# Six token tiles moved through DRAM with two block buffers and three landing buffers

## The chip, the cores and the metric

One core of a Trainium2 chip runs the whole program. The metric is the device time of one execution in microseconds (us). The engines are named as in the profile: PE (TensorE, the matrix engine), DVE (VectorE), ACT (ScalarE), POOL (GpSimd), and SP, whose queue issues all the DMAs of this kernel. Each engine works through its own instructions in the order in which they were recorded, and waits for others by semaphores.

## The reference

Three stages follow each other: attention, a first feed-forward layer with a softmax-like gate and a norm, and a mixture of four experts.

```python
scores = scale * q @ k^T          # 2 batches, 8 heads, 576 tokens, 64 wide
scores = where(mask, scores, -1e9)   # heads 0-3: a window of 32; heads 4-7: every 4th of 128
x = softmax(scores) @ v           # -> 1152 tokens x 512
h = x @ w_in                      # 512 -> 1024
e = exp(h - max(h));  solu = h * e / sum(e)
ln = (solu - mean) / sqrt(var + 1e-6) * g_ln
x = ln @ w_out                    # 1024 -> 512
for e in range(4):
    out += p[:, e] * (relu(x @ w1[e]) @ w2[e])   # 512 -> 1024 -> 512
```

All of it is float32; each product is made of three products of rounded parts (high x high, high x low, low x high).

## The kernel before

The 1152 tokens are nine tiles of 128 (t = 0 to 8) and three chunks of three tiles (c = 0 to 2). The work is cut into steps, each a Python generator that records a few instructions and yields. A long string, ORDER, names the step to be resumed next, up to the middle of the first expert; after that loops record the rest. So ORDER sets the order of every engine's instructions at once, and a "+" behind a name moves a choice from one engine to another (`copy`: ACT or, with +, DVE; `pick`: DVE or, with +, POOL; the last step of `moe_H`: DVE or, with +, ACT). The names used below:

- **UD.t.b, UP.t.b** (`att_U`): a block of attention; its scores and later "PV", the product with v, are PE work (lines 262, 271 and 320). Five of them carry the probabilities to DRAM and back in between (`da<-sta`, `pt<-da`, lines 299 and 303). After PV, `xhi` and `xlo` are written.
- **VO.j.t** (`conv_out`): converts w_out into `wh` and `wl`.
- **H.t** (`moe_H`): x @ w_in for one tile, 24 products in a `pm` tile of PSUM (line 350), then maximum, exponential, a product with sums and a scaling on DVE and ACT (lines 355 to 364). `pm` has two buffers, `pa` has two more.
- **T.t** (`moe_T`, `swap_T`): turns tile t so that its 1024 features lie on the partitions, and splits it into `hh` (high part, `copy`) and `hl` (low part, `pick`). Tiles 0 to 2 are turned on PE. Tiles 3 to 8 are turned in `swap_T`: DVE transposes blocks of 32x32 into `st4` (lines 395, 397), a DMA writes them to a DRAM tile `dt` (402, 405), DMAs read them back in another order into a landing buffer `et` (411, 414), ACT sums squares of `e` (407), and `hh` and `hl` follow (170 or 172, and 419). There is one `st4`, and a landing buffer for even and one for odd tiles. Tile 5 (`ROWS`) goes by four writes and one read, the other five by one write and two reads.
- **X.c.d** (`moe_X`): ln @ w_out for one chunk and one half of the outputs, 48 products in a `pm` tile (line 432) and a copy to `xf`. ORDER cuts the two X of chunk 0 in halves of 24, called X.0.0a, X.0.0b, X.0.1a and X.0.1b here. The first product of an X reads `hh` of its three tiles, the second one `hl`. Chunk 0 is tiles 0 to 2, chunk 1 tiles 3 to 5, chunk 2 tiles 6 to 8.
- **sc** (`scales`): small operations on the row sums, one of them on POOL (line 652).
- **XQ.s, WP.g, WV.g**: sums and splits of x, w1 and w2 for the experts (line 464 and the helper lines 170 and 172); **u.s** is the upward product of an expert in seven parts p1 to p7 (line 545), **d.t** the downward one (line 617). **l...** are loads.

`end_att` closes the attention's pools and opens `xf`, the pool of the last chunk's `hh` and `hl`, and the pool `spo` with `st4` and the landing buffers in their place.

Of the kernel before, what the change touches and what calls it, by code (L numbers as in the profile page):

```python
# [40 lines left out]
UP.2.1+ UP.2.1 H.4 H.4 UP.1.1+ VO.2.1+ UP.1.1+ UD.2.1+ UP.1.1 H.4 UP.1.1+ UP.1.1 UP.1.1 UP.1.1 X.0.1+ lO.3.0 VO.3.0 lvd.2.1 UP.2.1 VO.2.1+ UP.1.1+ VO.2.0+
VO.2.0 VO.2.1+ VO.2.1+ X.0.0 VO.3.0+ VO.3.0 VO.3.0+ VO.3.0 lO.3.1 VO.3.1 VO.3.1 UD.2.1+ VO.3.1+ VO.3.1 UP.2.1 VO.3.1 VO.3.0 H.4+ VO.3.1 VO.3.0+ VO.3.1 X.0.1+
UP.2.1 UP.1.1+ UP.1.1+ UD.2.1 UD.2.1 UP.1.1+ endA T.4 X.0.1 T.4+ T.4 H.3+ T.3+ T.3+ UP.1.1+ UP.1.1 H.5+ T.4+ T.3+ T.3+ H.5+ H.5+ H.5+ H.5+ H.5 X.0.0+ X.0.0
UP.2.1+ UP.2.1+ T.5+ T.5+ T.3+ H.6+ H.6+ T.4 T.4+ T.5 H.6 H.6+ T.3+ H.8 H.6 T.6 T.5+ T.6 H.8 H.8 T.5+ H.8+ H.8 T.8+ T.8+ T.6 T.6 H.7+ H.7 H.7 H.7 H.7 T.7+
# [9 lines left out]
def fused_kernel(ctx, tc, qkp, qkd, vp, vd, w_in, w_out, gp, w1, w2, out):  # L54
    nc = tc.nc
# [335 lines left out]
    def swap_T(t, e, lh, ll):  # L391
        ef = e.rearrange("p u x -> p (u x)")
        st = spo[0].tile([128, 4, 8, 32], F32, name="st4", tag="st4")
        if t in ROWS:
            nc.vector.transpose(st.rearrange("p g q j -> p q g j"), ef.rearrange("p (q g i) -> p q g i", g=4, i=32))
        else:
            nc.vector.transpose(st.rearrange("p (u g) q j -> p q u g j", u=2), ef.rearrange("p (q u i g) -> p q u g i", u=2, g=2, i=32))  # L397
# [2 lines left out]
        if t in ROWS:  # L400
            for g in range(4):
                nc.sync.dma_start(out=dt[32 * g:32 * g + 32, :].rearrange("i (a x) -> a i x", a=4), in_=st[:, g].rearrange("p q j -> p (q j)"))
        else:
            dw = dt.rearrange("p x -> (p x)").rearrange("(u p x) -> u p x", u=2, p=128)
            nc.sync.dma_start(out=dw.rearrange("u p x -> p u x"), in_=st.rearrange("p (u g) q j -> p u (g q j)", u=2))
# [381 lines left out]
```

## Time and profile before

| | us |
|---|---|
| median of three runs | 530.44 (529.91 to 531.85) |
| the profiled execution | 530.29 |
| its span, first to last instruction | 528.5 |
| PE busy in the span | 515.0 (97%), 3971 products |
| DVE, ACT, POOL busy | 356.9, 191.7, 187.3 |

The page gives PE a busy share near 100% in all but the first of its 40 slices, and in the chain of work that ended last PE holds 87% of the span and DMAs 7%. A time in the rows below is counted from the start of the span. PE's granted clock was 1.00 from 30 us on. How to read it: the loops of the experts fill the span from about 150 us to its end, and what comes ahead of them is a mixture of attention, conversions and the first layer in which all engines wait for each other.

### The profile page before, as it was taken

To read this page: it belongs to the slowest core of one execution; us is meant where nothing else is said; L and a number is where in the kernel's file an instruction comes from. 1 tells how busy PE (TensorE), PEld (TensorE's weight loads), DVE (VectorE), ACT (ScalarE), POOL (GpSimd) and SP (SyncE) were. 2 spreads that over 40 slices of the span, in tenths; PEclk is the share of its full clock that TensorE was granted. 3 is DMA by queue.
4 is the path that set the end of the run, shared out by engine and by line. 5 is a ranking of instruction groups with operands and counts; after the bars stand their busy time and mean duration, and the time that the engine had idled before them with its cause. 6 is when DMAs were issued, how large, how long until landed. Compare 5 with 4: busy or idle time off the path is not lost.

```text
span 528.5 us, 9419 instructions
## 1 busy us (share of the span) xinstructions
PE 515.0 (97%) x3971; PEld 459.0 (87%) x3971; DVE 356.9 (68%) x474; ACT 191.7 (36%) x295; POOL 187.3 (35%) x130
## 2 busy tenths in 40 slices
PE   7799999999999999999999999999999999999997
PEld 3578898888999998998989899898989889898986
DVE  6889996777978874854685485568448656853632
ACT  3768965423254432321422232142214213312210
POOL 2554220312233532730571173048117313820300
...
GB/s 311 364 239 211 242 175 97 112 141 211 16 159 141 19 2 35 126 1 1 159 1 1 0 160 0 1 141 20 2 0 161 1 0 81 0 1 1 1 81 99
DMA packets 24490, 46.44 MB, mean 88 GB/s; under 512 B 4480, under 2 KB 9088, under 8 KB 24064
## 3 DMA queue, kind: packets, MB, share of 16 engines
...
q8 instruction: 31, 0.51, 0.4%
...
## 4 chain that ended last, share of the span: by engine, by line
PE 87%; DMA 7%; DVE 4%; ACT 1%; SPq 1%; issue 0%; DVEq 0%; ACTq 0%
PE pa L617 19%; PE pm L617 18%; PE pm L545 17%; PE pa L545 17%; PE pm L350 7%; PE pm L432 6%; DMA vp<-in_vp_dram 2%; PE pa L320 2%; DMA et<-dt 2%; DMA draw<-in_moe_w_in_dram 1%; DMA dt<-st 1%; PE pa L271 1%; DVE e L359 1%; DVE e L364 1%; PE pa L381 1%; DVE st L397 0%
## 5 line engine op out<-in xcount | busy, mean ns | idle before, releaser
L558 DVE SCALAR_TENSOR_TENSOR hl<-ct,hh 128x512 fp32r<-128x512 f32 (+1 forms) x64 | 63.6, 1012 | 35.3 <-ACT hh L556 35.3
L556 ACT ACTIVATE hh<-ct 128x512 fp32r<-128x512 f32 (+1 forms) x64 | 42.1, 682 | 48.7 <-DVE ct L588 20.7
L617 PE MATMUL pa<-wl,hh 128*128 128x512 f32 (+1 forms) x148 | 57.3, 387 | 0.0
L617 PE MATMUL pa<-wh,hh 128*128 128x512 f32 (+1 forms) x148 | 57.3, 387 | 0.0
L617 PE MATMUL pa<-wh,hl 128*128 128x512 f32 (+1 forms) x148 | 57.1, 386 | 0.0
L545 PE MATMUL pm<-xoh,hl 128*128 128x256 f32 (+1 forms) x192 | 56.8, 296 | 0.0
L545 PE MATMUL pa<-xoh,hl 128*128 128x256 f32 (+1 forms) x192 | 56.8, 296 | 0.0
L545 PE MATMUL pm<-xol,hh 128*128 128x256 f32 (+1 forms) x192 | 56.8, 296 | 0.0
L545 PE MATMUL pa<-xol,hh 128*128 128x256 f32 (+1 forms) x192 | 56.8, 296 | 0.0
L545 PE MATMUL pm<-xoh,hh 128*128 128x256 f32 (+1 forms) x192 | 56.8, 296 | 0.0
L545 PE MATMUL pa<-xoh,hh 128*128 128x256 f32 (+1 forms) x192 | 56.8, 296 | 0.0
L617 PE MATMUL pm<-wl,hh 128*128 128x512 f32 (+1 forms) x144 | 55.7, 387 | 0.0
L617 PE MATMUL pm<-wh,hh 128*128 128x512 f32 (+1 forms) x144 | 55.7, 387 | 0.0
L617 PE MATMUL pm<-wh,hl 128*128 128x512 f32 (+1 forms) x144 | 55.6, 386 | 0.0
L464 POOL TENSOR_TENSOR wl<-wl,wh 128x1024 fp32r<-128x1024 f32 x7 | 16.9, 2414 | 95.3 <-ACT wh L172 95.3
L622 DVE SCALAR_TENSOR_TENSOR xf<-pm,pr,xf 128x512 f32<-128x512 f32 (+1 forms) x32 | 23.6, 738 | 31.1 <-PE pm L617 31.1
L464 POOL TENSOR_TENSOR hl<-sw,hh 128x512 fp32r<-128x512 f32 x22 | 33.5, 1522 | 30.3 <-ACT hh L172 27.6
L622 DVE SCALAR_TENSOR_TENSOR xf<-pa,pr,xf 128x512 f32<-128x512 f32 (+1 forms) x32 | 23.6, 738 | 30.3 <-PE pa L617 30.3
L172 ACT CAST wh<-wl 128x1024 fp32r<-128x1024 f32 x16 | 16.8, 1052 | 71.0 <-PE pa L617 40.5
L572 POOL TENSOR_TENSOR ct<-ct,ct 128x512 f32<-128x512 f32 (+1 forms) x15 | 21.4, 1426 | 48.1 <-ACT ct L570 42.9
L545 PEld LDWEIGHTS pm<-xoh,hh 128*128 128x128 f32 x192 | 36.4, 190 | 0.3
L545 PEld LDWEIGHTS pm<-xol,hh 128*128 128x128 f32 x192 | 36.4, 190 | 0.3
...
## 6 DMA issues: line engine op xcount, KB each, us to landing
wl<-in_moe_w_dram SPq DMA_DIRECT2D x16, 512.0 KB, 3.7
cvr<-in_moe_w_out_dram SPq DMA_DIRECT2D x8, 512.0 KB, 3.6
rw<-in_moe_w_dram SPq DMA_DIRECT2D x8, 512.0 KB, 6.0
wh<-in_moe_w_dram SPq DMA_DIRECT2D x8, 512.0 KB
...
dt<-st SPq DMA_DIRECT2D x5, 512.0 KB, 3.3
et<-dt SPq DMA_DIRECT2D x10, 256.0 KB, 4.2
```

Source lines behind the costliest of these rows:

```text
L172: nc.scalar.copy(out, in_)
L271: nc.tensor.matmul(ps[32 * g:32 * g + 32, j, 64 * m:64 * m + 64], lhsT=qt[rows, h, xq:xq + 32], rhs=kt[rows, h, xq:xq + 64], start=False, ...
L320: nc.tensor.matmul(po[64 * (g % 2):64 * (g % 2) + 64, j, o:o + 32], lhsT=vt[rows, m, g, :], rhs=pt[rows, m, g, :], start=True, stop=True)
L350: nc.tensor.matmul(pm[:, n, :], lhsT=xx[:, kk, cols], rhs=ww["in", kk][:, 512 * n:512 * n + 512], start=(n_ == 0 and i < 2), stop=(n_ == K ...
L432: nc.tensor.matmul(pm[:, dd, 0:CW], lhsT=w_, rhs=x_[:, f, :], start=(f == 0 and i == 0), stop=(f == KF - 1 and i == 2))
L464: pick().tensor_tensor(out=out, in0=a, in1=b, op=op)
L545: nc.tensor.matmul(ps[:, ff, 0:n], lhsT=a[:, kk, fc], rhs=b[:, kk, :], start=kk == 0 and m == 0, stop=kk == 1 and m == 2)
L556: nc.scalar.activation(out=hv, in_=src, func=AF.Relu)
L558: nc.vector.scalar_tensor_tensor(out=lv, in0=src, scalar=0.0, in1=hv.bitcast(F32), op0=ALU.max, op1=ALU.subtract)
L572: poolv().tensor_tensor(out=c12, in0=c21, in1=c22, op=ALU.add)
L617: nc.tensor.matmul(po[:, 0, 0:dn], lhsT=h_[:, f, cols], rhs=w_, start=(f == 0 and i == 0), stop=(f == 3 and i == 2))
L622: nc.vector.scalar_tensor_tensor(out=acc[:, t, dc], in0=po[:, 0, 0:dn], scalar=pr[:, t, e:e + 1], in1=acc[:, t, dc], op0=ALU.mult, op1=ALU ...
```

## The change

The row form of tile 5 is dropped (`ROWS` and its branches), so that all six tiles go by one write and two reads. `st4` becomes two buffers, `st40` and `st41`, and the landing buffers become three, `et0` to `et2`; both are given out in turn, whatever the tile's number (`turn`). `st40`, `et0` and `et1` lie in a new pool `spg`, which is open from the start; `st41` and `et2` lie in `spo`. ORDER is the same up to the step T.0 of its tenth line and another from there on; the main loops are untouched. A DMA scratch area is set to 1024.

```diff
-VO.1.0+ T.0 H.1+ lvp.2.1+ UD.2.1 lO.1.1+ UD.0.1+ T.0+ T.0 UD.1.1+ H.2+ H.2+ UD.2.1+ ...
+VO.1.0+ T.0 H.1+ lvp.2.1+ UD.2.1 lO.1.1+ UD.0.1+ T.0+ UD.1.1 UD.1.1 T.0 H.2+ UD.2.1 ...
...
-    spo = [None]
+    turn = [0, 0]
+    spo = [ctx.enter_context(tc.tile_pool(name="spg", bufs=1))]
...
-        st = spo[0].tile([128, 4, 8, 32], F32, name="st4", tag="st4")
-        if t in ROWS:
-            nc.vector.transpose(st.rearrange("p g q j -> p q g j"), ef.rearrange("p (q g i) -> p q g i", g=4, i=32))
-        else:
-            nc.vector.transpose(st.rearrange("p (u g) q j -> p q u g j", u=2), ef.rearrange("p (q u i g) -> p q u g i", u=2, g=2, i=32))
+        k = turn[0] % 2
+        turn[0] += 1
+        st = spo[k].tile([128, 4, 8, 32], F32, name=f"st4{k}", tag=f"st4{k}")
+        nc.vector.transpose(st.rearrange("p (u g) q j -> p q u g j", u=2), ef.rearrange("p (q u i g) -> p q u g i", u=2, g=2, i=32))
...
-        if t in ROWS:
-            for g in range(4):
-                nc.sync.dma_start(out=dt[32 * g:32 * g + 32, :].rearrange("i (a x) -> a i x", a=4), in_=st[:, g].rearrange("p q j -> p (q j)"))
...
-        et = spo[0].tile([128, 4, 256], F32, name=f"et{t % 2}", tag=f"et{t % 2}")
-        if t in ROWS:
-            nc.sync.dma_start(out=et.rearrange("p a x -> p (a x)"), in_=dt)
...
+        k = turn[1] % 3
+        turn[1] += 1
+        et = spo[k // 2].tile([128, 4, 256], F32, name=f"et{k}", tag=f"et{k}")
...
-        spo[0] = hp1.enter_context(tc.tile_pool(name="spo", bufs=1, side="right"))
+        spo.append(hp1.enter_context(tc.tile_pool(name="spo", bufs=1, side="right")))
...
-    nc = _bacc.Bacc("TRN2", target_bir_lowering=False, num_devices=1)
+    nc = _bacc.Bacc("TRN2", target_bir_lowering=False, num_devices=1, dynamic_dma_scratch_size=1024)
```

What the new ORDER does to the engines is seen in three places. In the changed file a line stands 1 to 7 lines higher (PV 319, the first layer 349, X 425, the block write 399, the read 407).

**PE, at the end of the attention.** `pt` are probabilities and `vp` values of a PV, `pm` is the PSUM tile that a row writes. Before, X.0.1b is followed by the PVs of UP.2.1 and UP.1.1, and then by H.5:

```order
L432 MATMUL pm_1232<-hl_943,wh7_1334 128x384
L432 MATMUL pm_1232<-hh_942,wl7_1335 128x384
L320 MATMUL pa_1365<-pt_1330,vp_954 64x32 x24
L320 MATMUL pa_1397<-pt_1392,vp_1075 64x32 x24
L350 MATMUL pm_1454<-wh0_206,xhi_90 128x512 x2
L350 MATMUL pm_1454<-wl0_207,xhi_90 128x512 x2
```

In the changed kernel the same place reads:

```order
L425 MATMUL pm_1236<-hl_946,wh7_1337 128x384
L425 MATMUL pm_1236<-hh_945,wl7_1338 128x384
L319 MATMUL pa_1399<-pt_1396,vp_1145 64x32 x24
L425 MATMUL pm_1274<-hh_945,wh6_1267 128x384
L425 MATMUL pm_1274<-hl_946,wh6_1267 128x384
```

The PV of UP.2.1 has moved ahead of X.0.1b, and X.0.0b (`pm_1274`), which stood behind H.5, now stands between the PV of UP.1.1 and H.5. H.6, H.8, H.7 and then X.1 follow in both.

**DVE, from the end of the attention to the block transpose of tile 5.** `e_1190` is tile 4, `e_1105` tile 3, `e_1486` tile 5. Before:

```order
L397 STREAM_TRANSPOSE st4_1441<-e_1190 128x8x4x32
L397 STREAM_TRANSPOSE st4_1448<-e_1105 128x8x4x32
L170 CAST xhi_90<-pa_1397 128x2x192
L246 TENSOR_TENSOR xlo_91<-pa_1397,xhi_90 128x2x192
L355 TENSOR_REDUCE nmx_83<-pm_1454 128x1
L359 SCALAR_TENSOR_TENSOR e_1486,nsum_85<-e_1486,pm_1454 128x1024
L364 TENSOR_SCALAR e_1486<-e_1486,nsum_85 128x1024
L170 CAST xhi_90<-pa_1365 128x2x192
L246 TENSOR_TENSOR xlo_91<-pa_1365,xhi_90 128x2x192
L395 STREAM_TRANSPOSE st4_1518<-e_1486 128x8x4x32
```

In the changed kernel (`e_1143` is tile 3, `e_1197` tile 4, `e_1515` tile 5):

```order
L169 COPY xf_1435<-pm_1236 128x2x384
L245 TENSOR_TENSOR xlo_94<-pa_1399,xhi_93 128x2x192
L169 COPY xf_1435<-pm_1274 128x2x384
L395 STREAM_TRANSPOSE st40_1497<-e_1143 128x8x4x32
L363 TENSOR_SCALAR e_1197<-e_1197,nsum_85 128x1024
L395 STREAM_TRANSPOSE st41_1503<-e_1197 128x8x4x32
L354 TENSOR_REDUCE nmx_83<-pm_1469 128x1
L245 TENSOR_TENSOR xlo_94<-pa_1340,xhi_93 128x2x192
L358 SCALAR_TENSOR_TENSOR e_1515,nsum_85<-e_1515,pm_1469 128x1024
L363 TENSOR_SCALAR e_1515<-e_1515,nsum_85 128x1024
L395 STREAM_TRANSPOSE st40_1521<-e_1515 128x8x4x32
```

The two copies of chunk 0 to `xf` came over from ACT, the two casts to `xhi` went there, and the scaling of tile 4 came over from ACT; nothing stands between the scaling of tile 5 and its transpose any more. Further on, the maximum of H.7 has moved ahead of the transpose of tile 8, and `sc` ahead of the splits of tiles 8 and 7.

**SP's queue, the DMAs of the six tiles** (the number behind `dt` is the tile). Before:

```order
L405 DMA dt4_1444<-st4_1441 128x2x512
L405 DMA dt3_1450<-st4_1448 128x2x512
L414 DMA et0_1467<-dt4_1444 64x4x256 x2
L414 DMA et1_1471<-dt3_1450 64x4x256 x2
L402 DMA dt5_1520<-st4_1518 4x32x256 x4
L411 DMA et1_1589<-dt5_1520 128x1024
L405 DMA dt6_1591<-st4_1587 128x2x512
L405 DMA dt8_1601<-st4_1599 128x2x512
L414 DMA et0_1604<-dt6_1591 64x4x256 x2
L405 DMA dt7_1639<-st4_1637 128x2x512
L414 DMA et0_1645<-dt8_1601 64x4x256 x2
L414 DMA et1_1709<-dt7_1639 64x4x256 x2
```

In the changed kernel:

```order
L399 DMA dt3_1499<-st40_1497 128x2x512
L399 DMA dt4_1505<-st41_1503 128x2x512
L407 DMA et0_1507<-dt3_1499 64x4x256 x2
L407 DMA et1_1512<-dt4_1505 64x4x256 x2
L399 DMA dt5_1523<-st40_1521 128x2x512
L407 DMA et2_1580<-dt5_1523 64x4x256 x2
L399 DMA dt6_1595<-st41_1593 128x2x512
L407 DMA et0_1632<-dt6_1595 64x4x256 x2
L399 DMA dt8_1635<-st40_1630 128x2x512
L399 DMA dt7_1667<-st41_1640 128x2x512
L407 DMA et1_1709<-dt8_1635 64x4x256 x2
L407 DMA et2_1715<-dt7_1667 64x4x256 x2
```

Tile 8 no longer lands in the buffer of tile 6, and the reads of tile 6 have moved ahead of the write of tile 8. Ahead of this place the queue has its loads in another order too: the read-back of UD.1.1 now stands behind three loads instead of two, and the load of `vp` for UP.1.1 further back. On POOL the order is nearly the old one up to the splits of tiles 3 to 5; POOL then takes the low part of tile 6, and makes two more low parts of the experts' operands and fewer of their sums.

## Rows read from the trace of the kernel before

**Rows 1.** Timeline of PE: start, us, instruction, count, [idle before <- releaser].

```profile
79.78 0.45 PE L432 MATMUL pm<-hh,wh 128*128 128x384 f32 x1
...
86.67 0.73 PE L350 MATMUL pm<-wh,xhi 128*128 128x512 f32 x2 [0.92 <-ACT xf L172]
...
92.24 0.33 PE L432 MATMUL pm<-hh,wh 128*128 128x384 f32 x1
...
96.43 0.62 PE L350 MATMUL pm<-wh,xhi 128*128 128x512 f32 x2
...
112.80 0.41 PE L432 MATMUL pm<-hh,wh 128*128 128x384 f32 x1
114.02 0.44 PE L432 MATMUL pm<-hl,wh 128*128 128x384 f32 x1 [0.82 <-POOL hl L419]
...
131.75 0.41 PE L432 MATMUL pm<-hh,wh 128*128 128x384 f32 x1 [0.98 <-ACT xf L172]
132.96 0.44 PE L432 MATMUL pm<-hl,wh 128*128 128x384 f32 x1 [0.80 <-DVE hl L419]
```

**Rows 2.** Timeline of ACT at the end of the attention.

```profile
85.81 0.80 ACT L172 COPY xf<-pm 128x768 f32<-128x768 f32 x1 [2.90 <-PE pa L320]
```

**Rows 3.** Timeline of DVE, 92 to 100 us and 115 to 117 us.

```profile
92.44 1.23 DVE L355 TENSOR_REDUCE nmx<-pm 128x1 f32<-128x1024 f32 x1 [1.43 <-PE pm L350]
...
97.94 1.24 DVE L395 STREAM_TRANSPOSE st<-e 128x1024 f32<-128x1024 f32 x1
99.09 2.70 DVE L170 CAST hh<-et 128x1024 fp32r<-128x1024 f32 x1
...
115.73 1.19 DVE L355 TENSOR_REDUCE nmx<-pm 128x1 f32<-128x1024 f32 x1
```

**Rows 4.** Timeline of SP's queue: start, us, line, DMA, count.

```profile
75.74 1.24 SPq L303 DMA_DIRECT2D pt<-da  x2
...
121.57 0.36 SPq L405 DMA_DIRECT2D dt<-st  x1
123.59 2.58 SPq L414 DMA_DIRECT2D et<-dt  x4
```

**Rows 5.** DMA issues in narrow stretches: count, KB each, us to landing.

```profile
dt<-st SPq DMA_DIRECT2D x1, 512.0 KB, 3.4
et<-dt SPq DMA_DIRECT2D x1, 256.0 KB, 4.1
et<-dt SPq DMA_DIRECT2D x2, 256.0 KB, 5.0
pt<-da SPq DMA_DIRECT2D x2, 96.0 KB, 2.7
pt<-da SPq DMA_DIRECT2D x1, 96.0 KB, 6.9
```

**Rows 6.** The chain that ended last, in order of time: start, us, what.

```profile
125.55 5.38 DMA et<-dt
```

**Rows 7.** Timeline of POOL at the splits of tiles 4 and 5 and at WP.0.

```profile
98.85 2.41 POOL L419 TENSOR_TENSOR hl<-et,hh 128x1024 fp32r<-128x1024 f32 x1 [25.30 <-ACT hh L172]
...
111.59 2.38 POOL L419 TENSOR_TENSOR hl<-et,hh 128x1024 fp32r<-128x1024 f32 x1 [7.31 <-DVE hh L170]
...
133.56 2.23 POOL L464 TENSOR_TENSOR sw<-rw,rw 128x512 f32<-128x512 f32 x1 [5.75 <-DMA rw<-in_moe_w_dram]
```

**Rows 8.** Timeline of DVE at the splits of tiles 6 and 7 and at XQ.0.

```profile
122.34 1.23 DVE L419 TENSOR_TENSOR hl<-et,hh 128x1024 fp32r<-128x1024 f32 x1
...
130.95 0.69 DVE L170 CAST hh<-et 128x1024 fp32r<-128x1024 f32 x1 [0.51 <-DMA et<-dt]
131.68 1.23 DVE L419 TENSOR_TENSOR hl<-et,hh 128x1024 fp32r<-128x1024 f32 x1
132.82 0.68 DVE L464 TENSOR_TENSOR ct<-xf,ct 128x512 f32<-128x512 f32 x1
...
134.56 2.38 DVE L464 TENSOR_TENSOR xol<-ct,xoh 128x512 fp32r<-128x512 f32 x2
```

More of the change, by code (lines that the diff above doesn't have):

```diff
@@ L41 @@
[L41 to L44, printed above, removed]
@@ L49 @@
-u.1+ WP.1+ u.1+ u.1+ u.1+ u.1 u.1+ d.1+ d.1 WP.1 WP.1 u.1 u.1 u.1 u.1+ WP.1 WP.1+ WP.1 WP.1 WP.1 WP.1 WP.1+ WP.1 d.3+ WP.1 WP.1+ WP.1 d.3 WP.1 u.1 u.1 u.1+
-u.1
+VO.1.0+ T.0 H.1+ lvp.2.1+ UD.2.1 lO.1.1+ UD.0.1+ T.0+ UD.1.1 UD.1.1 T.0 H.2+ UD.2.1 H.2+ T.1 T.1 UD.2.1+ T.0+ H.3 UD.2.1 lO.2.0+ T.1 T.1+ H.2 H.2 UD.0.1+
+VO.1.0 VO.1.1 VO.1.0 UP.2.1+ UP.2.1+ VO.1.1 VO.1.1+ lvd.2.1 UP.2.1 UD.0.1 H.2+ lP.1.1 UD.0.1+ UP.2.1 UD.1.1 UP.2.1+ UD.2.1+ UD.2.1+ UD.2.1+ H.3 VO.1.1 VO.2.0
+VO.1.1+ lO.2.1 VO.2.0 VO.2.0+ UD.2.1+ UD.1.1+ UD.1.1 UD.1.1 H.3+ lvp.1.1 T.2+ VO.2.0 UP.2.1 T.2+ VO.2.0+ lO.3.0+ VO.1.1 VO.1.1 T.2 T.2+ H.3+ H.3 UP.2.1+
@@ new lines @@
+UP.2.1+ UP.2.1+ H.4 H.4+ VO.2.1 VO.2.1+ VO.2.1 H.4 UP.1.1 UP.1.1+ VO.3.0 VO.2.1 UP.1.1+ UP.1.1 X.0.1 H.4+ UP.1.1 UP.1.1 UP.1.1 UP.1.1 VO.2.0 VO.2.0+ VO.2.1+
+VO.2.1 VO.2.1+ X.0.0 UD.2.1 VO.3.0 lO.3.1+ VO.3.0 VO.3.1+ VO.3.0+ VO.3.0 VO.3.1 VO.3.1+ VO.3.1 VO.3.1 UP.2.1 VO.3.0 UP.2.1+ VO.3.0 VO.3.1 VO.3.1+ X.0.1 UD.2.1
+UD.2.1 UP.1.1+ UP.1.1+ UP.1.1 UP.1.1 endA X.0.0 X.0.1+ UP.1.1+ X.0.0+ H.5+ H.5+ H.3+ T.3 T.3+ T.3+ H.4 T.4+ T.4+ T.3+ UP.2.1 T.4+ T.4 H.5 UP.2.1 H.5 H.5 H.5
+T.5+ T.5+ H.6 T.5 T.3+ T.3+ H.6+ H.8+ T.5 T.4+ H.6 H.6 H.6+ T.4+ H.8 H.8+ T.6 T.6+ T.5+ T.6+ T.5+ H.8+ H.7 H.7+ H.8+ H.7+ T.8+ T.6+ T.8+ T.8 H.7 H.7 T.7+
@@ new lines @@
+X.1.0 T.7+ T.7+ endH sc X.1.0+ T.8 T.8+ T.8 X.1.0+ T.7+ T.7+ T.7 X.1.1+ X.1.1+ T.6 XQ.0 X.1.1 XQ.0 XQ.0+ XQ.0 XQ.0+ XQ.0 XQ.0 lW.0 T.6+ XQ.0 XQ.0 WP.0 WP.0
+WP.0 WP.0 XQ.0 X.2.0 XQ.0 XQ.0+ WP.0 WP.0+ WP.0 WP.0+ WP.0 X.2.0 WP.0 WP.0 XQ.0+ XQ.0 XQ.0 XQ.0 X.2.1 XQ.1+ lV.0+ lW.1+ X.2.1 WP.0+ WP.0 u.0 WP.0 XQ.1 XQ.1
+XQ.1 WP.0 WP.0+ u.0 u.0 u.0 XQ.1 WP.0+ u.0 u.0+ u.0+ u.0 u.0 XQ.1 XQ.1 XQ.1 endX u.0+ XQ.1 XQ.1 WP.0 u.0+ u.0+ u.0 u.1 u.1+ u.0 u.0+ u.0 u.0 u.0+ lW.2 XQ.1+
+XQ.1 u.0 u.0+ u.0+ u.0 u.0+ u.0 u.1 WV.0 WV.0 WV.0 WV.0+ u.1+ u.1 u.1 u.1+ u.1+ u.1 u.1+ u.1 u.1 XQ.1+ u.1+ d.2 WP.1 u.1+ WP.1 XQ.1 d.3 d.3 XQ.1 d.2 WP.1
@@ L51 @@
+WP.1+ WP.1+ WP.1+ WP.1 WP.1+ WP.1 XQ.1 u.1+ u.1+ u.1 d.0+ d.1+ d.0 d.1+ WP.1 WP.1 u.1 u.1+ u.1 WP.1 WP.1 u.1 u.1+ u.1+ WP.1+ WP.1 WP.1+ WP.1 WP.1+ u.1 lV.1
 """
@@ L392, in swap_T @@
         ef = e.rearrange("p u x -> p (u x)")
[L393 to L397 removed]
+        k = turn[0] % 2
+        turn[0] += 1
+        st = spo[k].tile([128, 4, 8, 32], F32, name=f"st4{k}", tag=f"st4{k}")
+        nc.vector.transpose(st.rearrange("p (u g) q j -> p q u g j", u=2), ef.rearrange("p (q u i g) -> p q u g i", u=2, g=2, i=32))
         yield
         dt = dpo.tile([128, 1024], F32, name=f"dt{t}", tag=f"dt{t}")
[L400 to L405 removed]
+        dw = dt.rearrange("p x -> (p x)").rearrange("(u p x) -> u p x", u=2, p=128)
+        nc.sync.dma_start(out=dw.rearrange("u p x -> p u x"), in_=st.rearrange("p (u g) q j -> p u (g q j)", u=2))
         yield
@@ L408, in swap_T @@
         yield
-        et = spo[0].tile([128, 4, 256], F32, name=f"et{t % 2}", tag=f"et{t % 2}")
-        if t in ROWS:
-            nc.sync.dma_start(out=et.rearrange("p a x -> p (a x)"), in_=dt)
-        else:
-            for u in range(2):
-                nc.sync.dma_start(out=et[64 * u:64 * u + 64], in_=dw[u].rearrange("(a i) (g x) -> (i g) a x", a=4, g=2))
+        k = turn[1] % 3
+        turn[1] += 1
+        et = spo[k // 2].tile([128, 4, 256], F32, name=f"et{k}", tag=f"et{k}")
+        for u in range(2):
+            nc.sync.dma_start(out=et[64 * u:64 * u + 64], in_=dw[u].rearrange("(a i) (g x) -> (i g) a x", a=4, g=2))
         yield
```

8 lines of the change are left out of this document (removed).

## The prediction

> **What bounds the kernel now.** I read the busy shares first: PE is busy for 515.0 of 528.5 us, so a change that leaves PE's work alone can only win what PE stands idle. PE's timeline then shows where that is. The experts' loops from 150 us on run without a wait, and the attention's start, where PE waits for loads, is recorded before the point from which ORDER differs. Between lie four waits, at three places [rows 1]: 0.92 us ahead of H.5 (86.67), 0.82 us at the second product of X.1.0 (114.02), and 0.98 and 0.80 us at the first two products of X.2.0 (131.75, 132.96). They are 3.52 us together, and that is the most the change can bring.
>
> Next I asked who is late at each. H.5 needs a `pm` buffer, and both are held by X.0.0 and X.0.1; the copy that frees one starts only at 85.81, because `xf` lies in the attention's place and waits for the last PV [rows 2]. X.1.0 needs the low part of tile 5, which POOL makes from 111.59 for 2.38 us, that is until 113.97 [rows 7]. X.2.0 needs tile 7: its cast ends at 131.64 and its low part at 132.91 [rows 8], each just ahead of the product that waited (the profile names the copy to `xf`, which came much earlier, for the first of the two). The chain that ended last says the same: it goes through tile 7's read, issued at 125.55 and landing 5.38 us later [rows 6]. This read is the last of four that SP issues from 123.59 [rows 4]; the first two are tile 8's, and they had to wait until tile 6, in the same landing buffer, was split at 122.34 + 1.23 = 123.57 [rows 8].
>
> **The change, part by part.** PE's instructions are the same; what counts is when it may go on.
>
> *The seam at H.5.* PE was free at 86.67 - 0.92 = 85.75. In the new order X.0.0b stands there, which needs no new buffer. It lasts 96.43 - 92.24 = 4.19 us [rows 1], and under it the copy of X.0.1, which now goes to DVE, has 4 us for what took ACT 0.80 [rows 2]. So H.5 starts at 89.94 without a wait: minus 0.92. H.5 lasts 92.24 - 86.67 = 5.57 us and ends at 95.51 instead of 92.24; H.6, H.8 and H.7 last 112.80 - 96.43 = 16.37 us [rows 1], so X.1.0 could start at 111.88. DVE pays: its copy of X.0.0 waits until about 90.1 for PE, and the transposes of tiles 3 and 4 stand behind it. They are two of 1.24 us [rows 3] and a scaling, so DVE is free at about 94.3, before H.5's maximum at 95.7. Nobody needs tiles 3 and 4 before X.1.
>
> *Tile 5, the row form dropped.* Its maximum starts 92.44 - 92.24 = 0.20 us after H.5's end: 95.71. From there to the issue of the write I take 121.57 - 115.73 = 5.84 us, which is the unbroken chain of tile 7 [rows 3, 4]; before, tile 5's own was longer by the two steps of UP.2.1 that are now hidden. Write at 101.55; one of 512 KB lands after 3.4 us [rows 5]: 104.95. The second read is issued 2.58 / 4 = 0.65 us after the first [rows 4] and lands after 4.1 us [rows 5]: 109.7. A cast of 0.69 on DVE, which by its order is free then, and the 2.38 on POOL [rows 7, 8] give 112.85. So X.1.0's second product goes at about 112.9 instead of 114.02. PE still waits there, since H.5 came later while X.0.0b was put ahead of it: of the 0.82 us about half is left.
>
> *Tiles 6 to 8, three landing buffers.* From X.1.0's second product to the end of X.1 PE needs 131.75 - 0.98 - 114.02 = 16.75 us [rows 1], so X.2.0 is due at 129.65. Tile 7: H.7 ends at 111.88, its maximum now goes ahead of tile 8's transpose, at 112.1, and the write is issued 5.84 us later, at 117.9, instead of 121.57. It lands at 121.3. Tile 8 has a buffer of its own, so its reads are out by 119.6, and those of tile 7 are issued at 121.35 and 122.0. I take the longer landing, 5.0 us [rows 5], since they ran beside others: 127.0. Cast and low part, 0.69 + 1.23 [rows 8], end at 129.0, ahead of X.2.0's second product at 129.8. Tile 6's low part goes to POOL, behind `sc`; its reads are issued at about 112.5, so it has 10 us to spare. Both waits at X.2.0 go. What is late next is tile 7 itself, with 0.8 us in hand.
>
> *The rest of ORDER.* From X.2.0 on PE runs through in the trace of before. Both the operands' splits and PE's products move up by the same 3 us; the mix over DVE, ACT and POOL differs by a few steps. I cost it at nothing, and at the price of the second rival where the cover fails. Ahead of 85 us PE has no wait to win, so a change there can only cost: the PV of UP.2.1, moved ahead of X.0.1b, that is to 79.78 [rows 1], is the one step without long cover. Its second read is issued at 75.74 + 0.62 [rows 4] and lands after 2.7 us [rows 5], at 79.1, so there are 0.7 us in hand. The new pool and the scratch size issue no instruction.
>
> *The sum.* X.2.0's second product goes at 112.88 + 16.75 + 0.17 = 129.8 instead of 132.96, which is 3.2 us earlier, and all behind it follows. The profiled execution took 530.29 us, 0.15 less than the median: 530.29 - 3.2 = **527.1 us**, against the median a gain of 0.6%.
>
> *A row and a rule.* The cast of tile 3 took 2.70 us where that of tile 7 took 0.69; POOL worked from 98.85 to 101.26 beside it [rows 3, 7, 8]. The new order sets the cast of tile 4 beside POOL's part of tile 3, so it may take 2.7 again; H.6's product with sums, behind it on DVE, then frees `pm` for H.7 at about 106.4, just when PE asks for it. X.1.0 waits for tile 5 anyway, so the sum stays. By the Trainium skill, "SBUF — State Buffer", section "SBUF: two separate sides", DVE and GpSimd share a port pair that one of them holds for a whole instruction while the other is blocked. The trace agrees for this cast.
>
> **The rivals.** *First, tile 5 lands later.* Nothing but the landing of its reads stands between 112.9 and a longer wait. With 5.0 us instead of 4.1 [rows 5] X.1.0 goes on at 113.8 and the gain is 2.3: 528.0 us. For it: the reads of tile 4 run shortly before; against it: tile 6 writes only later. *Second, DVE and POOL get in each other's way at the experts' entry.* Before, two subtractions of XQ.0 took 2.38 us beside POOL's sum at 133.56, where one alone takes 0.68 [rows 7, 8]: one meeting costs 1.0 us. DVE has hardly idle time from there to the first u, and POOL has more low parts to make, one of them, for WV.0, of the 2.4 us kind, on which d.2 waits. By the rule above each such meeting blocks one of them outright. Two meetings more than before on the path cost 2.0: 529.1 us. Against it: PE did not wait once in this stretch before. *Third, the third buffer does not free the reads.* SP issues tile 8's reads behind tile 7's write, so they wait for it instead of tile 6's split. If DVE brings tile 7's transpose no earlier than before (write at 121.57), tile 7 lands again near 131 and X.2.0 waits as it did: about 530.0 us. It bites from a write later than 118.7. Against it: the maximum of H.7 was held up by DVE's order alone before. *Fourth, slower: PE stands at the PV of UP.2.1.* Its write to DRAM and its reads share the queue with loads that were moved. The longest such read took 6.9 us [rows 5]; landing then at 83.3 instead of 79.1 stops PE for 3.5 us, and if the write ahead of it is late by the same 6.9 - 2.7 = 4.2 us, for 7.7. I take the middle, 5.6: 530.29 - 3.2 + 5.6 = 532.7 us. It is slower than before from a stop of 3.2 us on. For it: PE has no wait ahead of this place that could absorb it; against it: the reads near 76 us, the same ones, took 2.7 before.
>
> **How the numbers follow.** The forecast gets 0.50, the first rival 0.16, the second 0.19, the third 0.08 and the fourth 0.07. About 0.5% (2.65 us, below 527.8) is what a measurement of this kernel can tell from no change, so the forecast counts as faster by only 0.7 us, and the first three rivals count as no change: faster 0.52, within 0.5% 0.43, slower 0.05. The low end is the bound of 3.52 us (526.8) less 0.4 for the spread of the runs, 526.4; the high end takes in the first two rivals with their spread, 529.5, and leaves out the last two.
>
> **What would show it.** In the profile after: no PE idle ahead of H.5, which starts near 89.9; X.1.0's second product near 112.9 behind POOL's low part; four reads in two pairs, tile 8's out before tile 7 has landed; tile 7's write near 117.9; X.2.0 near 129.7 without a wait; and u.0's first product 3 us earlier than before. I am wrong if PE waits newly at a PV near 80 us, at u.0, u.1 or d.2, or if tile 7's write stays near 121.

## The result, and the profile after

The changed kernel takes 526.04 us in the median of six executions (525.13 to 527.04), the kernel before in the same comparison 530.18; the ratio is 0.9917, with an interval from 0.9899 to 0.9935. Twelve more executions gave 526.41 and 0.9925 [0.9896, 0.9953]. The forecast was 527.1, its range began at 526.4: the direction is right, and the first six executions lie 0.4 us below the range, the later twelve at its end. The profiled execution took 526.39 us, with a span of 524.6.

PE of the changed kernel at the places of [rows 1] (start, us, instruction, [idle before <- releaser]):

```profile
61.05 1.07 PE L319 MATMUL pa<-pt,vd 64*64 64x32 f32 x48 [0.73 <-DMA pt<-da]
...
84.66 0.45 PE L425 MATMUL pm<-hh,wh 128*128 128x384 f32 x1
...
88.94 0.63 PE L349 MATMUL pm<-wh,xhi 128*128 128x512 f32 x2
...
110.96 0.33 PE L425 MATMUL pm<-hh,wh 128*128 128x384 f32 x1
111.74 0.44 PE L425 MATMUL pm<-hl,wh 128*128 128x384 f32 x1 [0.44 <-POOL hl L412]
...
129.25 0.41 PE L425 MATMUL pm<-hl,wh 128*128 128x384 f32 x1 [0.59 <-DVE hl L412]
```

X.0.0b stands at 84.66 and H.5 follows without a gap; 0.44 and 0.59 us are left at X.1.0 and X.2.0, and the PV of UD.1.1 waits newly for 0.73. SP's queue, to be read beside [rows 4]:

```profile
100.50 0.37 SPq L399 DMA_DIRECT2D dt<-st  x1
103.77 1.23 SPq L407 DMA_DIRECT2D et<-dt  x2
...
113.57 3.84 SPq L399 DMA_DIRECT2D dt<-st  x2
117.50 4.59 SPq L407 DMA_DIRECT2D et<-dt  x4
```

Tile 5 is written at 100.50 and its reads go at 103.77. Tiles 8 and 7 are written at 113.57 and about 117; tile 8's reads follow at once, tile 7's when its write has landed. POOL and DVE of the changed kernel at the splits of tiles 5 to 8, beside [rows 7, 8]:

```profile
109.29 2.40 POOL L412 TENSOR_TENSOR hl<-et,hh 128x1024 fp32r<-128x1024 f32 x1 [2.67 <-DVE hh L169]
...
120.75 2.42 POOL L412 TENSOR_TENSOR hl<-et,hh 128x1024 fp32r<-128x1024 f32 x1
```

```profile
120.82 2.37 DVE L646 SCALAR_TENSOR_TENSOR nmx<-nmx,esq 128x9 f32<-128x9 f32 x1 [2.01 <-POOL esq L645]
...
124.42 0.69 DVE L169 CAST hh<-et 128x1024 fp32r<-128x1024 f32 x1 [1.00 <-DMA et<-dt]
125.15 1.23 DVE L412 TENSOR_TENSOR hl<-et,hh 128x1024 fp32r<-128x1024 f32 x1
126.29 0.95 DVE L169 COPY xf<-pm 128x768 f32<-128x768 f32 x1
127.16 0.68 DVE L169 CAST hh<-et 128x1024 fp32r<-128x1024 f32 x1
127.88 1.23 DVE L412 TENSOR_TENSOR hl<-et,hh 128x1024 fp32r<-128x1024 f32 x1
```

Tile 8's cast waits for its landing. Tile 7's second read landed at 126.69, but its cast stands behind tile 8's split and a copy to `xf` and starts at 127.16; X.2.0 then waits for 0.59 us. In the three other traces of the changed kernel, taken for the experiments below, this wait is 0.68, 0.79 and none.

**Two traces, two halves.** I split each trace at two marks that both kernels have: the start of tile 2's transposes on PE ("T.2") and u.0's first product. T.2 starts at 63.06 us before and 62.05 after; from there to u.0 it is 86.48 and 83.77; from u.0 to the end 378.96 and 378.78. So 2.7 of the 3.9 us between the spans lie where the prediction had them, 0.2 behind u.0's start, and 1.0 ahead of T.2, where it had none.

The 0.2 us are not in the experts' loops: from u.0's first product to the last product of all it is 375.41 us before and 375.39 after. They lie behind the last product, 3.57 us before and 3.41 after, and go with the form of tile 5: all eight traces of kernels with the row form have 3.57 or 3.58 there, all ten with the block form 3.41 or 3.42. At its end SP waits for its DMAs' semaphores one after another. Before, the last output ends the first of four such waits, so that three more follow it; after, it ends the third, and one follows.

The stretch ahead of T.2 holds this (columns: stretch, its length, busy time and count of PE, PEld, DVE, ACT and POOL, PE's granted clock, DMA share, GB/s); before:

```profile
15.00:20.00 5.00, 4.15 (x61) 2.35 (x60) 3.61 (x9) 2.83 (x4) 3.42 (x3) 0.66 1.03 415
20.00:25.00 5.00, 3.65 (x100) 2.86 (x101) 4.63 (x9) 4.48 (x8) 2.61 (x1) 0.75 0.83 320
25.00:30.00 5.00, 4.70 (x112) 3.94 (x111) 3.68 (x6) 3.40 (x6) 3.17 (x1) 0.91 0.80 278
```

and after:

```profile
15.00:20.00 5.00, 3.99 (x79) 2.74 (x81) 4.83 (x10) 3.94 (x6) 3.32 (x3) 0.66 1.02 410
20.00:25.00 5.00, 3.65 (x92) 2.77 (x88) 3.96 (x9) 3.94 (x5) 2.62 (x1) 1.00 0.86 322
```

Both kernels have the same instructions here, yet before PE's clock is at its lower level (1.2 of 2.4 GHz) for a part of 20 to 30 us too. In the changed kernel PE was as little busy from 20 to 25 us (3.65 of 5 us) at a granted clock of 1.00, so that busy share alone does not explain it.

### The profile page after: what moved, and what is told of

Same layout as the page of the kernel before. It is cut to its first block, busy times and chain, and to the rows that moved or that the text cites. A ratio compares the mean times of both kernels' runs of the same rounds, so it can differ in the third digit from the quotient of the medians.

```text
span 524.6 us, 9409 instructions
## 1 busy us (share of the span) xinstructions
PE 512.2 (98%) x3965; PEld 457.9 (87%) x3971; DVE 353.9 (67%) x474; ACT 190.2 (36%) x294; POOL 190.8 (36%) x131
## 4 chain that ended last, share of the span: by engine, by line
PE 91%; DMA 6%; DVE 2%; ACT 0%; SPq 0%; issue 0%; ACTq 0%; DVEq 0%
PE pa L610 19%; PE pm L610 18%; PE pm L538 17%; PE pa L538 17%; PE pm L349 9%; PE pm L425 6%; DMA vp<-in_vp_dram 2%; PE pa L319 2%; DMA draw<-in_moe_w_in_dram 1%; DMA et<-dt 1%; DMA pt<-da 1%; PE pa L270 1%; PE pa L380 1%; DVE hl L412 0%; DVE hh L169 0%
## 5 line engine op out<-in xcount | busy, mean ns | idle before, releaser
L551 DVE SCALAR_TENSOR_TENSOR hl<-ct,hh 128x512 fp32r<-128x512 f32 (+1 forms) x64 | 61.8, 986 | 34.8 <-ACT hh L549 34.8
L457 POOL TENSOR_TENSOR wl<-wl,wh 128x1024 fp32r<-128x1024 f32 x8 | 19.4, 2424 | 97.6 <-ACT wh L171 97.6
L457 POOL TENSOR_TENSOR hl<-sw,hh 128x512 fp32r<-128x512 f32 x24 | 36.5, 1526 | 49.7 <-ACT hh L171 48.6
L538 PEld LDWEIGHTS pa<-xoh,hh 128*128 128x128 f32 x192 | 36.4, 190 | 0.3
```

The source lines that it names most:

```text
L457: pick().tensor_tensor(out=out, in0=a, in1=b, op=op)
L538: nc.tensor.matmul(ps[:, ff, 0:n], lhsT=a[:, kk, fc], rhs=b[:, kk, :], start=kk == 0 and m == 0, stop=kk == 1 and m == 2)
L551: nc.vector.scalar_tensor_tensor(out=lv, in0=src, scalar=0.0, in1=hv.bitcast(F32), op0=ALU.max, op1=ALU.subtract)
```

## The experiments

**Is the earlier start of T.2 the change's doing?** The scratch size and the pool that is open from the start are all that could act there without ORDER. First the scratch size alone, in the kernel before:

```diff
-    nc = _bacc.Bacc("TRN2", target_bir_lowering=False, num_devices=1)
+    nc = _bacc.Bacc("TRN2", target_bir_lowering=False, num_devices=1, dynamic_dma_scratch_size=1024)
```

> The kernel before with nothing changed but the DMA scratch size of 1024. In the two profiles the first 52 us, whose instructions stand in the same order in both kernels, are 1.7 us shorter after the change, and the granted clock is at half (0.50) once more before, from 22.7 to 25.6 us. Theory 1 (the scratch size or the early pool is the cause): if it is the scratch size, this kernel is 1.5 to 2 us faster than the kernel before, with a second product of T.1's place at about 51.9 us instead of 53.5. Theory 2 (chance: the half-clock spell comes and goes between executions of one kernel): within 0.5 us of the kernel before, and the mean granted clock of its runs spreads as widely as that of the kernel before.

Measured: 528.40 us, ratio 0.9970 [0.9946, 0.9993]. T.2 started at 62.71. Then with the one block buffer and the two landing buffers in a pool open from the start as well:

```diff
-    spo = [None]
+    spo = [ctx.enter_context(tc.tile_pool(name="spg", bufs=1))]
...
-        spo[0] = hp1.enter_context(tc.tile_pool(name="spo", bufs=1, side="right"))
```

> The kernel before with the scratch size of 1024 and its one block buffer and two landing buffers in a pool that is open from the start, instead of one that opens at the end of the attention; order and row form as before. Theory 1 with the early pool as the cause: 1.5 to 2 us faster than the kernel before, all of it ahead of 55 us. Theory 2: no change ahead of 55 us beyond the spread between executions; the waits at H.5, X.1.0 and X.2.0 stay (0.9, 0.8, 1.8 us), so within 0.5 us of the kernel before.

Measured: 530.60 us, ratio 0.9997 [0.9972, 1.0022], T.2 at 62.02. Since the second kernel contains the first edit and gains nothing, the two edits together bring no gain; the 0.3% of the first alone stays unexplained. The trace of the first, with the scratch size alone, showed one thing more, PE's clock behind the waits of X.2.0:

```profile
130.00:135.00 5.00, 3.82 (x14) 3.58 (x15) 4.97 (x6) 2.50 (x4) 1.49 (x1) 0.74 0.31 116
135.00:140.00 5.00, 5.00 (x28) 5.00 (x28) 4.28 (x7) 1.23 (x2) 1.29 (x1) 0.92 0.00 0
```

**The new wait at UD.1.1.** The edit takes the changed kernel and moves two loads (`vd`, `qkP`) behind the read-back of UD.1.1:

```diff
-... UP.2.1+ lvd.2.1 UP.2.1 UD.0.1 H.2+ lP.1.1 UD.0.1+ UP.2.1 UD.1.1 UP.2.1+ ...
+... UP.2.1+ UP.2.1 UD.0.1 H.2+ UD.0.1+ UP.2.1 UD.1.1 lvd.2.1 lP.1.1 UP.2.1+ ...
```

> The changed kernel with the two loads of vd and qkP that stand ahead of the read-back of UD.1.1 moved behind it on SP's queue. Theory: the new wait of 0.73 us at the PV of UD.1.1 comes from these loads, beside which the two reads took 4.6 to 5.0 us to land; without them they land in about 3.5 us, the wait is gone and the kernel is 0.5 to 0.8 us faster than the changed kernel (about 525.4 us). Rival: the load of cvr alone fills the DMA engines there, the reads land as late, and nothing changes (526.0 us).

Measured: 525.76 us, ratio 0.9909 [0.9879, 0.9938], not to be told from the changed kernel. The wait is gone from UD.1.1 and stands at UD.0.1 (56.14, 1.07 us, again for `pt<-da`). That the edit moved it is not shown: of the three other traces of the changed kernel two have neither wait and the third one of 0.27 us at UD.0.1, so such waits come and go. The DMAs are busy here (a mean share of 0.91 from 45 to 60 us in the changed kernel).

**Tile 8's reads ahead of tile 7's write.**

```diff
-X.1.0 T.7+ T.7+ endH sc X.1.0+ T.8 T.8+ ...
+X.1.0 T.8 T.7+ T.7+ endH sc X.1.0+ T.8+ ...
```

> The changed kernel with tile 8's two reads ahead of tile 7's write on SP's queue. Theory: the 0.59 us that PE still waits at X.2.0 come from tile 8, whose reads were issued at 117.5 and 118.1, behind tile 7's write, and shared the DMA engines with it: 5.9 to 6.2 us to landing. Issued first they land in about 4 us, at 121; then only tile 7 is late, its write goes about 0.8 us later, and X.2.0 starts without a wait: 0.4 to 0.6 us faster than the changed kernel (about 525.5). Rival: tile 7's later write makes it land as late as the two do now, 0 to 0.4 us slower.

Measured: 528.57 us, ratio 0.9961 [0.9937, 0.9984]; X.2.0 waited for 0.87 and 0.78 us again. SP's queue shows why:

```profile
117.15 1.23 SPq L407 DMA_DIRECT2D et<-dt  x2
118.47 0.56 SPq L399 DMA_DIRECT2D dt<-st  x1
123.87 1.23 SPq L407 DMA_DIRECT2D et<-dt  x2
```

Tile 7's write, beside tile 8's reads, took 5.3 us to land, where in the changed kernel it took 3.8, and it was issued 0.9 us later, counted from T.2; tile 7's reads came 5.4 us behind it. The path is tile 7's write, as the rival had it, but the loss is larger than its 0.4 us: 2.2 us against the twelve executions of the changed kernel.

**Which part of the change carries the gain?** The changed kernel again for more executions, its buffers with the old ORDER, the new ORDER without them:

> The changed kernel once more, for more executions of it. Theory 1, the sum of the steps as the two traces show them: 1.2 us up to X.1.0, 1.4 us at X.2.0 and 0.2 us behind it, 2.8 us in all, which is a ratio of 0.9947; the first measurement, 0.9917, would then have had about 1.6 us of luck in it. Theory 2: the trace of before had its attention late by chance and so hid a wait that the new order takes away as well (PE ahead of tile 2's transposes, for H.2's exponential, 0.7 to 1.0 us); then the gain is 3.5 to 4 us in every set of executions, a ratio of 0.992 to 0.9935, and the trace shows no wait for H.2 ahead of tile 2's transposes, near 62 us.

> The changed kernel's buffers and its form of tile 5 with the old ORDER. Theory 1, the buffers carry what they stand for: tile 5 lands some 3 us earlier, so the 0.82 us at X.1.0 go; tile 8's reads no longer wait for tile 6's split and are issued right behind tile 7's write, near 121.6, tile 7's own reads near 125.0 when that write has landed, alone, so they land near 129.7 instead of 130.9 and X.2.0 waits for 0.6 to 0.8 us instead of 1.78; the 0.92 us at H.5 stay. Gain 1.8 us, ratio about 0.9966. Rival, the order carries it: tile 8's reads share the DMA engines with tile 7's write, it lands 2 us later, and X.2.0 waits as before: gain 0.8 us, ratio about 0.9985.

> The kernel before, with one block buffer, two landing buffers and the row form of tile 5, and the new ORDER. Theory 1: the order alone wins the 0.92 us at H.5 and the wait for H.2 (0.7 us), but tile 5 by rows lands as late as it did, so X.1.0 waits for 1.5 us or more, and tile 8's reads wait for POOL's low part of tile 6 (near 123) with tile 7's reads behind them, which land near 130: X.2.0 waits for 1.5 us or more. Gain at most 1 us, ratio 0.998 to 1.0. Rival, the order carries it all: ratio below 0.995 and waits at X.1.0 and X.2.0 below 0.8 us each.

And each half of the buffers' edit alone, with the old ORDER (`ROWS` emptied; or two block and three landing buffers with tile 5 in row form):

```diff
-ROWS = (5,)
+ROWS = ()
```

> The kernel before with one edit: tile 5 goes by one write and two reads like the others. One block buffer, two landing buffers, the old ORDER. Theory 1, the row form is what held up DVE, and with it all that comes behind tile 5: in the trace of before DVE waits 0.82 us for tile 5's write ahead of tile 6's transpose (107.47) and 0.98 us for tile 5's landing ahead of the product of H.8 (110.81). Both waits go, so X.1.0 has no wait, and tile 7's write is issued about 1.8 us earlier against H.5; tile 8's reads still wait for tile 6's split, so X.2.0 keeps 0.5 to 1.3 us of its 1.78. Gain 1.3 to 2.1 us and more where other waits shrink: ratio 0.993 to 0.9975. Rival, X.2.0 needs the third landing buffer: only the 0.82 us at X.1.0 go, ratio 0.9985, and X.2.0 waits for 1.6 us or more.

> The other half: two block buffers and three landing buffers, with the old ORDER and tile 5 by four writes and one read as before. Theory 1 (the row form held up DVE): DVE still waits for tile 5's landing, near 110 us, only the wait for the block buffer goes; tile 8's reads no longer wait for tile 6's split. X.1.0 waits as before (0.8 us), X.2.0 for about 1 us instead of 1.78: ratio 0.998 to 0.999. Rival, the buffers carry it: X.2.0 waits for 0.6 us or less, ratio 0.9965 or below.

The same two edits undone under the new ORDER:

```diff
-        k = turn[1] % 3
+        k = turn[1] % 2
```

> The changed kernel with two landing buffers given out in turn instead of three; ORDER, block form and block buffers stay. Theory 1, as the prediction has it: tile 8's reads then wait for tile 6's low part, which POOL ends near 123.2, and tile 7's reads stand behind them and land near 129 instead of 127; X.2.0 waits for about 2 to 2.5 us instead of 0.6, which is 1.5 to 2 us more than the changed kernel: ratio 0.9955 to 0.9965. Rival: the reads are not what tile 7 waits for, ratio as the changed kernel's, 0.9925.

> The changed kernel with tile 5 by four writes and one read again; new ORDER, two block and three landing buffers stay. Theory 1, the row form is the dear part: it takes 8 to 9 us from the write's issue to the read's landing here instead of about 7, and DVE stands at tile 5's cast; X.1.0's second product waits for 3 us or more instead of 0.4, H.7 is late, and X.2.0 with it: ratio 0.998 or above. Rival, with the buffers there the form hardly matters: ratio below 0.995.

Measured ("T.2 to u.0" from the traces; the first row is the mean of five, of the kernel before and of the two variants above, the last one of four of the changed kernel; the first median is that of all 84 executions of the kernel before):

| ORDER | tile 5 | block, landing buffers | T.2 to u.0, us | median, us | ratio to before |
|---|---|---|---|---|---|
| old | rows | 1, 2 | 86.73 | 529.8 | 1 |
| old | rows | 2, 3 (o_bufs) | 85.78 | 529.40 | 1.0006 [0.9983, 1.0029] |
| old | block | 1, 2 (o_block5) | 85.20 | 527.55 | 0.9967 [0.9947, 0.9987] |
| old | block | 2, 3 (a_oldorder) | 83.75 | 526.70 | 0.9923 [0.9895, 0.9951] |
| new | rows | 1, 2 (b_neworder) | 95.17 | 537.44 | 1.0141 [1.0093, 1.0188] |
| new | rows | 2, 3 (a_row5) | 89.09 | 532.67 | 1.0070 [1.0036, 1.0104] |
| new | block | 2, 2 (a_et2) | 85.05 | 527.70 | 0.9975 [0.9952, 0.9998] |
| new | block | 2, 3 (the change) | 83.62 | 526.41 | 0.9925 [0.9896, 0.9953] |

The rows with a label have one trace each; the five traces of the first row lie between 86.24 and 87.48, the four of the last between 83.23 and 83.82.

The new ORDER is worth 0.1 us on the traces and nothing that the runs can tell (a mean of 526.4 us in twenty executions against 526.5 in the eight of a_oldorder); the buffers and the block form under the old ORDER bring all the gain that can be told. Theory 1 for a_oldorder was too low by half, its rival by more. Theory 1 for a_same, a gain of 2.8 us, lies within this run's interval, but outside that of the first comparison; the wait for H.2, its theory 2, is taken up further below. The two single edits came out as their theory 1 had it, the buffers alone with no gain that the runs can tell (0.9 us in the one trace); a_et2 lost 1.3 us where 1.5 to 2 were expected, a_row5 more than I had thought. PE with the old ORDER and the new buffers:

```profile
61.91 1.09 PE L381 MATMUL pa<-ident,e 128*128 128x128 f32 x8 [0.29 <-ACT e L362]
...
85.49 0.74 PE L350 MATMUL pm<-wh,xhi 128*128 128x512 f32 x2 [0.92 <-ACT xf L172]
...
129.08 0.45 PE L426 MATMUL pm<-hl,wh 128*128 128x384 f32 x1 [0.47 <-DVE hl L413]
```

The 0.92 us at H.5 stay, but X.1.0 does not wait and X.2.0 only for 0.47. I had expected waits of 0.6 to 0.8 there. Tile 7's write goes at 118.61, where before it went at 121.57 [rows 4], counted from T.2 1.8 us earlier, although no step of ORDER moved. The new ORDER sends it 1.7 us earlier still, and nothing is left of that at tile 7's cast, 65.16 us after T.2 here and 65.11 in the changed kernel: there the write took 3.8 us instead of 2.9 and the second read 5.2 instead of 4.8, and the copy to `xf` stands ahead of the cast. What the row form costs is in the chain that ended last of the kernel before, between the rows that I had read:

```profile
101.02 6.33 DMA dt<-st
...
107.50 3.29 DMA et<-dt
...
110.81 0.70 DVE hh L170
111.51 1.15 DVE e L359 x2
...
112.69 1.85 DVE e L364
...
114.56 1.25 DVE st L397
115.80 1.12 DVE nmx L355
...
120.30 1.25 DVE st L397
```

Tile 5's write (101.02) and read (107.50) end in its cast on DVE at 110.81, and from there the chain goes on DVE through H.8's product and scaling, tile 8's transpose, H.7's maximum and, after the exponential on ACT, to tile 7's transpose (120.30), with no wait for anything else. The landing of tile 5 sets the start of tile 7's write. In block form the cast stands at 107.79, counted from T.2 1.2 us earlier and from H.5 1.8, and DVE does not wait for it (old ORDER, one block buffer):

```profile
107.79 0.69 DVE L170 CAST hh<-et 128x1024 fp32r<-128x1024 f32 x1
109.18 1.22 DVE L359 SCALAR_TENSOR_TENSOR e<-e,pm 128x1024 f32<-128x1024 f32 x1 [0.70 <-ACT e L357]
...
110.44 1.07 DVE L364 TENSOR_SCALAR e<-e,nsum 128x1024 f32<-128x1024 f32 x1
```

Of the 1.8 us that tile 7's write gains against H.5 (which starts at 85.47 here), 1.05 come from the earlier start of H.8's scaling and 0.77 from the scaling itself: it takes 1.07 us where it took 1.84. Before, tile 5's late landing had set it beside POOL's low part of tile 5 (111.59 to 113.97); alone such a scaling takes 0.75.

Why the row form lands late shows in the DMA engines (columns as above, the last two the share of the sixteen DMA engines and GB/s). The first line is tile 5's four writes before, from the last issue to the landing, the second one the middle of its one write in the changed kernel:

```profile
101.10:107.30 6.20, 6.20 (x29) 5.13 (x28) 3.91 (x5) 1.21 (x2) 2.55 (x2) 1.00 0.25 80
101.30:102.70 1.40, 1.40 (x8) 1.17 (x7) 1.40 (x2) 0.79 (x3) 1.40 (x1) 1.00 0.95 350
```

The four writes keep a quarter of the DMA engines' time busy, the one write nearly all of it. The two forms differ in the number of writes, in the length of their pieces (1 KB against 2 KB) and in how the pieces lie in `dt`; no run parts these.

With the buffers and the row form DVE's wait for tile 5 is about as long as its two waits before together (0.82 us for the block buffer and 0.98 for the landing), and PE waits at X.1.0 too (o_bufs, DVE and PE):

```profile
109.83 0.69 DVE L170 CAST hh<-et 128x1024 fp32r<-128x1024 f32 x1 [1.95 <-DMA et<-dt]
```

```profile
113.09 0.44 PE L435 MATMUL pm<-hl,wh 128*128 128x384 f32 x1 [0.86 <-POOL hl L422]
131.05 0.44 PE L435 MATMUL pm<-hl,wh 128*128 128x384 f32 x1 [0.80 <-DVE hl L422]
```

The block form removes the first wait and moves all behind it; the third landing buffer then removes most of the second. Without it (a_et2) PE stands at X.2.0 for 1.60 us, nearly as before, which bears out the third buffer's part in the prediction; 2 to 2.5 us were expected for this run:

```profile
128.35 0.41 PE L425 MATMUL pm<-hh,wh 128*128 128x384 f32 x1 [0.81 <-PE pm L425]
129.54 0.41 PE L425 MATMUL pm<-hl,wh 128*128 128x384 f32 x1 [0.79 <-DVE hl L412]
```

The new ORDER, in turn, needs the block form, since it puts X.0.0b ahead of H.5 and so starts tile 5 later. By rows (a_row5) DVE stands for tile 5, and PE behind it:

```profile
115.08 0.69 DVE L169 CAST hh<-et 128x1024 fp32r<-128x1024 f32 x1 [5.40 <-DMA et<-dt]
```

```profile
117.06 0.41 PE L434 MATMUL pm<-hh,wh 128*128 128x384 f32 x1 [4.14 <-DVE e L358]
```

With one block buffer besides (b_neworder) tile 4's transpose waits for tile 3's write (3.17 us at 95.05), H.7 for 2.32 us and X.2.0 for 3.11. My expectation for that run, a gain of up to 1 us, was far off: I had priced the waits at X.1.0 and X.2.0 one by one, and not DVE's queue behind tile 5.

**Does a wait cost more than its length?** Tile 7's split is made twice on DVE, with the same result:

```diff
+        if t == 7:
+            nc.vector.tensor_copy(out=lh, in_=ev)
+            nc.vector.tensor_tensor(out=ll, in0=ev, in1=lh.bitcast(F32), op=ALU.subtract)
         copy(lh, ev)
```

> The changed kernel with tile 7's split made twice on DVE, 0.69 + 1.23 us more behind its landing; nothing else differs. X.2.0 then waits for about 2.4 us instead of 0.6. Theory 1, a wait of PE costs its own length: 1.8 us more than the changed kernel, ratio 0.995 to 0.996. Theory 2, a wait of this length at this place also takes PE's clock down for a stretch behind it, as one trace showed (granted clock 0.74 from 130 to 135 us, 1.6 us lost): 3 to 3.5 us more, ratio 0.998 to 0.999, with a granted clock well below 1 in the trace behind X.2.0.

Measured: 528.88 us, ratio 0.9983 [0.9957, 1.0008], that is 2.5 us more than the changed kernel beside it. PE waited as intended:

```profile
131.37 0.41 PE L428 MATMUL pm<-hh,wh 128*128 128x384 f32 x1 [1.70 <-ACT xf L171]
132.57 0.41 PE L428 MATMUL pm<-hl,wh 128*128 128x384 f32 x1 [0.78 <-DVE hl L415]
```

From T.2 to u.0 it is 85.53 us, 1.9 more than the changed kernel's mean, and the granted clock behind the wait is 1.00 throughout; so in this trace the wait cost its length. The ratio lies in theory 2's range, but its interval reaches into theory 1's, and the 2.5 us lie between the two; the question stays open. Over the timed executions the mean granted clock was 0.9956 here and 0.9972 in the changed kernel beside it, so some may have had what the trace did not; the trace cannot show which.

**Head or clock?** Two more traces of each kernel:

> The kernel before once more, for its trace alone. Theory 1, the share of the gain that is no shorter wait between tile 2's transposes and the first u is clock: the traces of before then show stretches of a low granted clock more often, also behind the waits of X.2.0 (130 to 140 us), and tile 2's transposes start between 61 and 64 us as in the changed kernel. Theory 2, it lies in the head: tile 2's transposes start 1 us later in before than in the changed kernel, on the mean of the traces, 62.6 against 61.6.

> As the run before it, another trace of the kernel before: theory 1, tile 2's transposes within 61 to 64 us and low granted clock in some stretch; theory 2, tile 2's transposes at 62.6 us or later.

> The changed kernel, for its trace alone. Theory 1: tile 2's transposes between 61 and 64 us, no low granted clock behind X.2.0. Theory 2: tile 2's transposes at 61.6 us or earlier.

> As the run before it, another trace of the changed kernel: theory 1, tile 2's transposes between 61 and 64 us; theory 2, at 61.6 us or earlier.

T.2 started at 62.46 and 61.12 in the kernel before (529.65 and 529.39 us), at 60.84 and 62.07 in the changed one (525.09 and 525.88). Each program by itself spreads over 1.6 to 1.9 us (before 61.12 to 63.06, changed 60.51 to 62.07). Over all traces the mean start is 62.05 us in the eight with the old ORDER and 62.03 in the ten with the new one: no effect of ORDER on the head can be seen. The two kernels' own traces do differ, 62.21 in the mean of three against 61.37 of four, but by less than each spreads, so theory 2 is not borne out; nor is that of a_same: the new ORDER has no wait for H.2, and starts T.2 no earlier for it. Neither new trace of before had a low clock behind X.2.0, so of theory 1 only the half on the head is borne out by them, with the 60.84 just below its 61.

The clock of every execution is recorded, and within one program the time falls with it: over 219 executions, each program with a level of its own, 0.001 of mean granted clock is 0.34 us (standard error 0.03). The kernel before had 0.9952 in the mean, the changed one 0.9969 (the difference has a standard error of 0.0007): an estimate of 0.6 us by that slope, which shows that time and clock go together and not which moves the other.

## Why the prediction was wrong

The changed kernel's mean lies 3.8 us under that of before (530.2 in 84 executions, 526.4 in 20). The traces give 3.0 us from T.2 to u.0 (83.62 us against 86.65, the mean of the four traces in the table's first row without the low clock shown above) and 0.2 behind the last product; the clock gives an estimated 0.6, which no trace shows at a place of its own. The prediction had 3.2, all of it ahead of u.0.

**Right.** The three places, the block form's chain and the landing buffer. Counted from T.2, H.5 was forecast at 26.88 us and stands at 26.89; X.1.0's second product at 49.82, and it is 49.69. Tile 5's write follows its maximum by 5.88 us (5.84 were taken), lands in 3.3 and its reads in 3.7. Tile 4's cast took 2.04 us beside POOL, where 2.7 had been allowed. (By its own terms the prediction's end of tile 5's low part is 112.77, not 112.85; nothing hangs on the 0.1 us.) PE did not stand at the PV of UP.2.1, and nothing behind X.2.0 got in the way: X.2.0's second product to u.0 lasts 16.6 us in both traces. So no rival came in: tile 5 did not land late, and tile 7's write went 54.99 us after T.2 (54.84 were forecast), ahead of the point from which the third rival decides.

**Mis-sized.** "What is late next is tile 7 itself, with 0.8 us in hand": it was late by 0.59 us. I had let tile 8's reads go by because they were issued early. They took 5.9 us beside tile 7's write, and tile 8's split and a copy of 0.95 us stand ahead of tile 7's on DVE, so the cast began at 127.16 instead of about 126. Some 0.7 us of that is the landing (126.69, with its write 0.4 us and its read 0.2 us longer than taken), the rest DVE.

**Wrong: which part earns what.** I gave the seam's 0.92 us and the early maximum of H.7 to the new ORDER. This step failed: the buffers and the block form with the old ORDER reach u.0 as early (83.75 us after T.2 against 83.62), and the new ORDER without them loses 7.6 us. Of the seam's gain some 0.3 us arrive at X.1.0 (49.56 us after T.2 in the mean, 49.86 in the one trace of a_oldorder), where PE then waits for tile 5, which X.0.0b had put back; and tile 7 comes early because tile 5 no longer holds DVE; the further 1.7 us that the new ORDER wins at its write are lost again before its cast. I read the chain of before only at tile 7's read [rows 6] and treated tile 5 as a matter of X.1.0 alone.

**Wrong: the low end.** "They are 3.52 us together, and that is the most the change can bring." This step set the low end of the range. The waits of one trace are no bound, though the 3.0 us between T.2 and u.0 stay within it. PE is also slower where its clock is low, and that is no idle time in any row: an estimated 0.6 us, as above. The end behind the last product became 0.2 us shorter, and "ahead of 85 us PE has no wait to win" holds only for the trace that I read, one with T.2 at 63.06; in six of the eight old-ORDER traces PE stood there for 0.3 to 1.0 us for H.2's exponential. That did not matter in the end: the new ORDER avoids this wait, in six of its ten traces it stands for a read-back near it instead, and the mean start of T.2 is the same. The remaining 0.3 us between the forecast and the six executions are within the difference between the two sets of the same program (526.04 and 526.41). Not settled is why the kernel before had the lower mean clock: a stretch at the lower level behind X.2.0's waits was seen in one of the five traces of the table's first row, that with the scratch size. Longer waits had one behind them (3.11 us in b_neworder, then 0.67 from 135 to 140 us; 4.14 us in a_row5, then 0.79 from 115 to 120 us), the wait made on purpose (1.70 and 0.78 us) had none.
